# Reordering the seam between linear attention and a mixture of experts: gathers, u-term sums, copies and logits

## The chip, the cores and the metric

The kernel runs on one core of a Trainium2 chip. A core has TensorE (PE in the profile, its weight loads PEld), VectorE (DVE), ScalarE (ACT), GpSimd (POOL) and SyncE (SP), each with its own queue of instructions, and 16 DMA engines. The metric is the device time of one execution in microseconds. The times of the kernel before are 598.85, 599.25 and 601.51 us, the median 599.25.

## What is computed

A linear attention over 4 batches, 8 heads, 768 steps and 48 channels makes 3072 tokens of width 384; these go through a mixture of 8 experts, two of them for each token. Cut to what matters:

```python
for t in range(S):                                    # attention, w and u per head and channel
    cur = einsum('bhd,bhe->bhde', u * k_t, v_t)       # the u-term
    y[:, :, t] = einsum('bhd,bhde->bhe', r_t, state + cur)
    state = w * state + einsum('bhd,bhe->bhde', k_t, v_t)
x = y.transpose(0, 2, 1, 3).reshape(B * S, H * D)     # 3072 x 384

noisy = x @ w_gate + log1p(exp(x @ w_noise)) * noise  # routing
top2 and their softmax weights per token
for e in range(8):                                    # each token through its two experts
    out[token] += weight * (relu(x[token] @ w1[e]) @ w2[e])
```

## The kernel before

**Attention.** The loop at L1329 runs over 24 tiles of 128 tokens (6 chunks of time by 4 batches). Tile i goes through `products` (POOL: the u-term product rku of tile i+1, L410 to L421, and the scaled keys kd of tile i+2, L402), `ystate` and `yout` (PE: state and value parts of py, L531; the logits of tile i-1, L569; from tile 13 on the u-term sums of tile i+1, L433), `kvup` and `zup_v` (the state), `uterm_b` (DVE: the u-term sum c, L444 or L442, and its product cv with the values), `xout` (DVE: x = py + cv, L560, and its store to DRAM, xd), `turn_kr` (PE: turns of k and r of tile i+2, L225; DVE rT, ACT kT), `scores` (PE: PAB, L476), `turn_x` (PE turns x into KX, L225; ACT copies it to xT, L470) and `mask` (DVE: am, L484).

**Routing.** The logits are read in two groups of 12 tiles. A generator `route(g)` makes the top two, their slots and gates in some hundred small DVE steps; `steps(n)` and, later, `rstep(us)` issue a few of these between the other work, so where they are called sets the order on DVE, ACT and PE. Lists of token rows come from small PE matmuls (`place`, L709) behind two ACT scalings (L700); `rstep` counts down two calls from a list's making: the scaling at the first, the matmuls at the second. `rows` turns a list into row numbers GR (L883 to L885). `maybe_early`, at the end of a tile, does this for the first three token tiles of expert 0 once group 0 is routed, and `xgather` at once issues three indirect DMAs on POOL that gather them (L1020). All engines run their queue in order, so what stands behind a gather on POOL waits for it.

**Experts.** At the last tile `xT_first` (L1057) turns the three gathered tiles on PE (into RV, PAB and RT), with `turn_x` of tile 23 between the second and third, and then makes all three ACT copies xh (L1076) and three DVE remainders xl (L1078). `p1` is the first product of a chunk (ph, 8 blocks of 9 matmuls, L1132, with ACT and DVE making hb and ht, L1136 and L1138), `p2` the second (pym, L1168). Expert 0's first chunk is `p1(0, 0)`: its first four matmuls are issued at L1389, then `pl_alone` issues the logits of tile 23 into pl (L569), then the rest follows. The second chunk of expert 0 (s = 1 at L1469) carries the last routing steps: after each block of nine matmuls `rstep(STEPS_L0)`, then `wstep`, a step of the weight loading. Expert 1's gathers (list_1, L1432) and its turns (ptm, L1049) follow from these. From about 200 us on the experts follow each other with no routing between them.

Of the kernel before, what the change touches and what calls it, by code (L numbers as in the profile page):

```python
# [35 lines left out]
STEPS_L0 = 0.9  # L36
# [20 lines left out]
def kernel(  # L57
# [999 lines left out]
    def xT_first(between):  # L1057
        xh = moe.tile([128, ND, WMAX], F32R, name="xh")
        xl = moe.tile([128, ND, WMAX], F32R, name="xl")
        XH[0, 0] = (xh, xl)  # L1060
        part = lambda x, t: by_row(x[:, :, t * 128:(t + 1) * 128])
        whole = RT[:, :ND * 128].rearrange("p (d t) -> p d t", d=ND)
        ts = []
        for t, dst in zip(chunks(0)[0], (RV, PAB, None)):
            if dst is None:
                between()
            for d in range(ND):
                xg = XG[0, t][:, d * 128:(d + 1) * 128]
                if dst is None:
                    nc.tensor.transpose(whole[:, d, :], xg, ident)  # L1070
                else:
                    turn_rows(dst, d * 64, xg)
            ts.append((t, whole, xh[:, :, t * 128:(t + 1) * 128], xl[:, :, t * 128:(t + 1) * 128]) if dst is None else
                      (t, halves_of(dst, 0, ND), part(xh, t), part(xl, t)))
        for _, x, h_, l_ in ts:
            nc.scalar.activation(h_, x, AF.Copy)  # L1076
        for t, x, h_, l_ in ts:
            nc.vector.tensor_sub(l_, x, h_.bitcast(F32))  # L1078

# [30 lines left out]

    nph = [0]

    def p1(e, ci):
        w_ = sum(tw(t) for t in chunks(e)[ci])
        xh, xl = XH[e, ci]
        wh, wl = W[e][0]
# [5 lines left out]
        for f in range(NF):  # L1122
# [7 lines left out]
                q.sort(key=lambda z: z[1] is xl)  # L1130
            for j, (a, x, d) in enumerate(q):
                nc.tensor.matmul(ph[:, :w_], a[:, d, fs], x[:, d, :w_], start=(j == 0), stop=(j == len(q) - 1))  # L1132
                if nph[0] == 1 and j == 3:
                    yield
            for h_, a, b in parts:
                nc.scalar.activation(h_[:, f, 0, :], ph[:, a:b], AF.Relu)  # L1136
            for h_, a, b in parts:
# [157 lines left out]
                return  # L1295
            credit[0] -= c or 0.25

    def early(g):
        rows(EARLY[g] // 128, EARLY[g + 1] // 128, rows_of(g))
        xgather(0, g, g)  # L1300

    def route_when_done(i):
        for g, (a, b) in enumerate(GROUPS):
# [17 lines left out]

    def maybe_early():
        if 0 in routed and not late_mm and not early_done:
            early(0)
            early_done.append(1)

    early_done = []
    flag = consts_c()
    for i in range(NT):  # L1329
        products(i)  # L1330
        if i + 5 < NT:
            load(i + 5, (0, 2))
        if i in (4, 6):
# [16 lines left out]
        uterm_c(i, CV_EARLY, H)  # L1350
        steps(2)
        tick()
        if i + 1 < NT:
            uterm_b(i + 1)
        steps(1)
        xout(i)
        while i == I_EARLY and not early_done:
            rstep(1)
            maybe_early()
        if i == NT - 1:  # L1360
            logits_out(i - 1)
            route_when_done(i - 1)
            steps(3)
            xT_first(lambda: turn_x(i))
            p1a = p1(0, 0)
        else:
            turn_kr(i + 2)
            if i:
                logits_out(i - 1)
                route_when_done(i - 1)  # L1370
            uterm_c(i + 1, 0, CV_EARLY)
            steps(1)
            scores(i + 1)
            turn_x(i)
            tick()
            steps(1)
            mask(i + 1)
            steps(3)
            maybe_early()
        if not i:  # L1380
# [5 lines left out]
    psm[0] = ps_pool(ps_left, "psm", "left")  # L1386
    att_stack.close()
    hbp[0] = stack.enter_context(tc.tile_pool(name="hbp", bufs=1, side="right", reuse_waits="tile"))
    next(p1a)  # L1389
    ps_right.close()  # L1390
    psr[0] = ps_pool(ps_right, "psr", "right")

# [76 lines left out]
    for s in range(1, len(seq)):  # L1469
# [11 lines left out]
            xh_, xj_ = xD(*seq[s + 1]) if not end else ([], [])  # L1481
        else:
            xt = xT(*seq[s + 1])
        for j, _ in enumerate(p1(e, ci)):
            while hold and (s > 1 or listed):
                emit_out(*hold.pop(0))
            if s == 1:
                rstep(STEPS_L0)
                wstep()
                continue  # L1490
            if s > 2:
# [164 lines left out]
```

## Time and profile before

| | before |
|---|---|
| median of three | 599.25 us |
| the profiled execution | 599.14 us |
| its span, first to last instruction | 597.40 us |
| busy in the span: PE, PEld, DVE, ACT, POOL | 572.5, 547.3, 347.0, 284.8, 277.9 us |
| mean granted TensorE clock | 0.982 |

The rows quoted below are from that profiled execution, and times in them are microseconds from the span's start. A timeline row gives start, length, engine, line, operation, output<-inputs, shapes and count, and in brackets the idle time before it with what ended it. The attention ends and the experts start at about 136 us. A line without an entry in brackets followed its predecessor with hardly a gap.

### The profile page before, as it was taken

Reading aid. Unit: us, or ns where it says so; the run is one execution under the profiler, and the core shown is the slowest. Engines: PE = TensorE matmul, PEld = TensorE weight load, DVE = VectorE, ACT = ScalarE, POOL = GpSimd, SP = SyncE. Lnnn points to the kernel's source line nnn. Section 1 sums busy time; section 2 is a strip of 40 time slices with the busy share of each in tenths; the row PEclk is TensorE's granted clock in tenths of the full one; section 3 lists DMA queues with packets and bytes.
Section 4 is the critical chain, followed back from the end, with each engine's and each line's share of the span. In section 5 each row is a group of like instructions: output and inputs, shape, how many; then the busy total and the mean of one; then the engine's idle time right before and its main releaser. Section 6 shows DMA issues by size and latency. Waiting matters only on the chain.

```text
span 597.4 us, 13911 instructions
## 1 busy us (share of the span) xinstructions
PE 572.5 (96%) x5383; PEld 547.3 (92%) x5384; DVE 347.0 (58%) x788; ACT 284.8 (48%) x712; POOL 277.9 (47%) x416
## 2 busy tenths in 40 slices
PE   8899899969999999999999999999999999999995
PEld 5899888858898999999999999999999999999995
DVE  5998798837766455546454645455454546455331
ACT  4358777823263443554445545554554454445220
POOL 8998656640243743345352633344343516333222
PEclk9899999968999999999999999999999999999998
DMA  9998998219332661775654645565756455434211
GB/s 172 203 220 175 225 220 204 73 54 279 103 110 67 201 220 53 161 217 135 146 170 116 184 115 166 130 183 108 182 124 176 143 146 154 139 93 84 67 35 41
DMA packets 143225, 86.53 MB, mean 145 GB/s; under 512 B 118624, under 2 KB 133215, under 8 KB 143152
## 3 DMA queue, kind: packets, MB, share of 16 engines
q1 hardware_dynamic: 132368, 56.76, 39.6%
q0 software_dynamic: 10160, 28.81, 15.9%
q8 instruction: 44, 0.72, 0.5%
q14 instruction: 29, 0.24, 0.1%
q10 hardware_dynamic: 624, 0.00, 0.1%
HBM read 58.81 MB, written 19.86 MB: 132 GB/s over the span
## 4 chain that ended last, share of the span: by engine, by line
PE 86%; DVE 5%; issue 4%; POOL 3%; ACT 1%; DMA 1%; POOLq 0%; ACTq 0%; DVEq 0%
PE ph L1132 34%; PE pym L1168 32%; PE py L531 5%; PE PAB L476 3%; PE KX L225 2%; PE pym L1161 2%; PE pym L1159 2%; PE py L569 1%; DVE am L484 1%; POOL GT L1027 1%; PE RV L494 1%; PE RV L225 1%; PE RV L182 1%; PE ptm L1049 1%; DVE x L560 1%
## 5 line engine op out<-in xcount | busy, mean ns | idle before, releaser
L1168 PE MATMUL pym<-w1h,hb 128*128 128x384 f32 x768 | 200.4, 337 | 0.0
L1168 PEld LDWEIGHTS pym<-w1h,hb 128*128 128x128 f32 x768 | 139.4, 188 | 0.2
L1138 DVE SCALAR_TENSOR_TENSOR hb<-ph,hb 128x384 fp32r<-128x384 f32 x128 | 71.2, 556 | 117.4 <-ACT ht L1136 76.1
L1132 PE MATMUL ph<-xh,w0h 128*128 128x384 f32 (+1 forms) x384 | 136.2, 355 | 1.3 <-ACT xh L1076 1.3
L1132 PE MATMUL ph<-xh,w0l 128*128 128x384 f32 (+1 forms) x384 | 135.5, 353 | 0.0
L1132 PE MATMUL ph<-xl,w0h 128*128 128x384 f32 (+1 forms) x384 | 129.8, 352 | 0.0
L1168 PE MATMUL pym<-w1l,hb 128*128 128x384 f32 x384 | 129.2, 337 | 0.0
L1136 ACT ACTIVATE hb<-ph 128x384 fp32r<-128x384 f32 x128 | 62.9, 491 | 105.4 <-PE ph L1132 105.3
L1193 POOL DMA_INDIRECT out_dram<-ot,TK x56 | 60.3, 1076 | 105.7 <-DVE ot L1187 55.0
L1020 POOL DMA_INDIRECT xg<-xd,GR x56 | 60.7, 1083 | 59.1 <-DVE r_e L603 25.9
L1132 PEld LDWEIGHTS ph<-xh,w0h 128*128 128x128 f32 x384 | 72.5, 189 | 5.0 <-ACT xh L1076 1.6
L1132 PEld LDWEIGHTS ph<-xh,w0l 128*128 128x128 f32 x384 | 72.6, 189 | 3.1
L1132 PEld LDWEIGHTS ph<-xl,w0h 128*128 128x128 f32 x384 | 72.1, 188 | 3.3
L1168 PEld LDWEIGHTS pym<-w1l,hb 128*128 128x128 f32 x384 | 72.1, 188 | 0.1
L1035 POOL DMA_INDIRECT pv<-out_dram,GA x49 | 48.8, 997 | 48.3 <-DMA out_dram<-ot,TK 35.6
L1106 ACT ACTIVATE xh<-xj 128x384 fp32r<-128x384 f32 (+1 forms) x42 | 21.1, 502 | 43.8 <-DVE xj L1104 43.5
L1176 ACT ACTIVATE ot<-pym 128x384 f32<-128x384 f32 x42 | 20.4, 486 | 40.6 <-PE pym L1168 33.8
L1107 DVE TENSOR_TENSOR xl<-xj,xh 128x384 fp32r<-128x384 f32 (+1 forms) x42 | 22.4, 534 | 24.8 <-ACT xh L1106 24.8
L1092 ACT ACTIVATE pl<-xg 128x768 uint16<-128x768 uint16 (+1 forms) x42 | 35.3, 841 | 0.9 <-DMA xd<-pl 0.9
L484 DVE TENSOR_TENSOR am<-PAB,mneg 128x512 int32<-128x512 int32 x48 | 30.8, 683 | 5.3 <-PE PAB L476 5.0
L476 PE MATMUL PAB<-rT,kT 64*128 64x128 f32 x384 | 28.7, 286 | 2.9 <-issue 2.5
L402 POOL TENSOR_TENSOR kd<-kt,tabk 128x192 f32<-128x192 f32 x46 | 28.1, 631 | 4.9 <-DMA kt<-in_k_dram 2.1
(276 smaller groups left out, 837.6 us busy)
## 6 DMA issues: line engine op xcount, KB each, us to landing
stg<-in_moe_w_dram SPq DMA_DIRECT2D x24, 512.0 KB, 4.6
stg<-in_moe_w_dram SPq DMA_DIRECT2D x32, 384.0 KB, 3.4
xd<-x SPq DMA_DIRECT2D x24, 196.0 KB, 3.5
rd<-in_r_dram SPq DMA_DIRECT2D x24, 192.0 KB, 4.3
vt<-in_v_dram SPq DMA_DIRECT2D x24, 192.0 KB, 4.4
out_dram<-ot SPq DMA_DIRECT2D x16, 288.0 KB, 4.2
kt<-in_k_dram SPq DMA_DIRECT2D x23, 192.0 KB, 4.0
xg<-xd,GR POOLq DMA_INDIRECT x56, 3.1
```

The source lines that it names most:

```text
L402: nc.gpsimd.tensor_mul(KD[i][:, h], kt[i][:, h], tabk[:, h, :D])
L476: nc.tensor.matmul(pa[:, s, p, :], kT[i][s * 64:(s + 1) * 64, p, :], rT[i][s * 64:(s + 1) * 64, p, :], start=True, stop=True)
L484: nc.vector.tensor_tensor(am[:, :, h].bitcast(I32), pa[:, :, h].bitcast(I32), mneg[:, None].to_broadcast([128, 2, NP // 2, 128]), op=ALU.b ...
L531: nc.tensor.matmul(o[qs], lhsT[:, qs], rhs, start=first[q], stop=last, skip_group_check=True)
L1020: nc.gpsimd.indirect_dma_start(out=xg[:n, :XW if e else DM], out_offset=None, in_=xd[:rows_of(early_)], in_offset=bass.IndirectOffsetOnAxi ...
L1035: nc.gpsimd.indirect_dma_start(out=pv[:n], out_offset=None, in_=out, in_offset=bass.IndirectOffsetOnAxis(ap=GA[:n, e * NJ + t:e * NJ + t + ...
L1092: nc.scalar.activation(pl[:n], XG[e, t][:n, :DM].bitcast(U16).rearrange("p (d two) -> p two d", two=2), AF.Copy)
L1132: nc.tensor.matmul(ph[:, :w_], a[:, d, fs], x[:, d, :w_], start=(j == 0), stop=(j == len(q) - 1))
L1136: nc.scalar.activation(h_[:, f, 0, :], ph[:, a:b], AF.Relu)
L1138: nc.vector.scalar_tensor_tensor(h_[:, f, 1, :], ph[:, a:b], 0.0, h_[:, f, 0, :].bitcast(F32), op0=ALU.max, op1=ALU.subtract)
L1168: nc.tensor.matmul(py, hb[:, f, a, hs], x[:, f, :], start=(j == 0), stop=(j == len(q) - 1))
L1193: st = nc.gpsimd.indirect_dma_start(out=out, out_offset=bass.IndirectOffsetOnAxis(ap=TK[:n, q:q + 1], axis=0), in_=ot[:n], in_offset=None, ...
```

## The change

Five edits, all of order:

- `maybe_early` makes the row numbers only; the three early gathers are issued after `products` of the next tile (tile 22 here).
- `uterm_b` of tile 1 stands behind `mask` of tile 1, not ahead of `xout` of tile 0. All other tiles keep their place.
- In `xT_first` each ACT copy xh is issued right behind its tile's turns.
- `next(p1a)` is gone: the logits of tile 23 come before the first matmul of `p1(0, 0)`.
- `p1` takes a call `mid`, made behind the fifth of nine matmuls. For s = 1 it is half a routing step, and the step at the block's end is halved too.

```diff
-        for _, x, h_, l_ in ts:
-            nc.scalar.activation(h_, x, AF.Copy)
+            nc.scalar.activation(ts[-1][2], ts[-1][1], AF.Copy)
...
-    def p1(e, ci):
+    def p1(e, ci, mid=lambda: None):
...
-                if nph[0] == 1 and j == 3:
-                    yield
+                if j == 4:
+                    mid()
...
-    def early(g):
-        rows(EARLY[g] // 128, EARLY[g + 1] // 128, rows_of(g))
-        xgather(0, g, g)
...
-            early(0)
+            rows(EARLY[0] // 128, EARLY[1] // 128, rows_of(0))
             early_done.append(1)
...
         products(i)
+        if early_done and (0, 0) not in XG:
+            xgather(0, 0, 0)
...
-        if i + 1 < NT:
+        if i and i + 1 < NT:
             uterm_b(i + 1)
...
+        if i == I_EARLY and (0, 0) not in XG:
+            xgather(0, 0, 0)
...
             mask(i + 1)
+            if not i:
+                uterm_b(i + 1)
...
-    next(p1a)
...
-        for j, _ in enumerate(p1(e, ci)):
+        for j, _ in enumerate(p1(e, ci, lambda: rstep(STEPS_L0 / 2)) if s == 1 else p1(e, ci)):
...
             if s == 1:
-                rstep(STEPS_L0)
+                rstep(STEPS_L0 / 2)
```

On POOL at the end of tile 21 and the start of tile 22, the difference of the two orders (kd are scaled keys, xg<-xd the three early gathers, w1l the low half of expert 0's second weights, rku the u-term product of tile 23):

```order
 L421 TENSOR_TENSOR rku<-rT,kT 128x256 x2
 L402 TENSOR_TENSOR kd_101<-kt,tabk 128x4x48 x2
+L359 TENSOR_TENSOR w1l_1337<-stg,w1h_1336 128x384
+L421 TENSOR_TENSOR rku<-rT,kT 128x256 x2
 L1020 DMA xg<-xd,GR 128x384 x3
-L359 TENSOR_TENSOR w1l_1337<-stg,w1h_1336 128x384
-L421 TENSOR_TENSOR rku<-rT,kT 128x256 x2
 L356 TENSOR_TENSOR w1l_1337<-stg,w1h_1336 128x384
 L359 TENSOR_TENSOR w1l_1337<-stg,w1h_1336 128x384
```

The gathers have moved behind one weight half and the rku of tile 23; two weight halves stay behind them.

On ACT at the last tile, before (lg are logits, xT the turned tile 23, xh the copies of the gathered tiles):

```order
L578 ACTIVATE lg<-py 128x16
L470 ACTIVATE xT<-KX 128x2x3x64
L1076 ACTIVATE xh<-RV 128x2x3x64
L1076 ACTIVATE xh<-PAB 128x2x3x64
L1076 ACTIVATE xh<-RT 128x3x128
L578 ACTIVATE lg<-pl 128x16
```

and after:

```order
L578 ACTIVATE lg<-py 128x16
L1075 ACTIVATE xh<-RV 128x2x3x64
L1075 ACTIVATE xh<-PAB 128x2x3x64
L470 ACTIVATE xT<-KX 128x2x3x64
L1075 ACTIVATE xh<-RT 128x3x128
L578 ACTIVATE lg<-pl 128x16
```

The copy of tile 23 has moved behind two of the three xh copies. On PE the matmuls of pl (L569), which stood behind the first four of ph, now stand ahead of all of them.

On DVE at tile 0, the difference (z is the state, c and cv the u-term of tile 1, x of tile 0, rT of tile 2, am the mask of tile 1):

```order
 L504 TENSOR_TENSOR z_214<-RV,w_176 128x192
-L444 TENSOR_REDUCE c_365<-rku 128x8
-L448 TENSOR_TENSOR cv<-vt,c_365 128x384
 L560 TENSOR_TENSOR x_146<-py,cv 128x384
 L464 TENSOR_TENSOR rT<-RV,pwr 128x2x4x64
 L484 TENSOR_TENSOR am<-PAB,mneg 128x2x256 x2
+L444 TENSOR_REDUCE c_406<-rku 128x8
+L448 TENSOR_TENSOR cv<-vt,c_406 128x384
```

The sum and the product of tile 1 have moved behind the x of tile 0 and the mask of tile 1. The order of SP is the same in both.

## Rows read from the trace of the kernel before

**Rows 1.** Windows: stretch, length; busy (instructions) PE PEld DVE ACT POOL; PEclk, DMA share, GB/s.

```profile
16.40:20.00 3.60, 3.49 (x66) 3.33 (x66) 3.56 (x9) 0.49 (x1) 3.60 (x7) 0.54 1.02 220
...
119.73:125.41 5.68, 0.00 (x1) 0.00 (x0) 0.21 (x2) 0.46 (x3) 4.78 (x6) 0.74 0.37 104
125.41:132.70 7.29, 7.21 (x100) 6.91 (x101) 3.86 (x12) 2.90 (x11) 2.57 (x3) 0.50 0.08 30
132.70:136.20 3.50, 2.03 (x41) 1.53 (x39) 2.00 (x7) 1.82 (x5) 0.00 (x0) 0.99 0.33 67
136.20:139.50 3.30, 3.25 (x19) 2.70 (x20) 1.16 (x4) 0.18 (x1) 0.00 (x0) 0.50 1.00 282
139.50:151.30 11.80, 11.80 (x72) 11.64 (x71) 11.08 (x43) 3.44 (x7) 0.00 (x0) 1.00 0.97 300
```

**Rows 2.** Waits of PE over the span: us in total, times, longest.

```profile
PE py L433 <- POOL rku L421: 5.7, 1, 5.7
PE KX L225 <- DVE x L560: 3.3, 3, 2.5
...
PE ptm L1049 <- DMA xg<-xd,GR: 1.2, 1, 1.2
```

**Rows 3.** POOL timeline at tile 22, and the landing times of all gathers.

```profile
119.99 1.15 POOL L1020 DMA_INDIRECT xg<-xd,GR  x1 [4.29 <-DVE r_e L600]
...
122.71 0.94 POOL L1020 DMA_INDIRECT xg<-xd,GR  x1 [0.30 <-issue]
...
124.63 1.40 POOL L421 TENSOR_TENSOR rku<-rT,kT 128x256 f32<-128x256 f32 x2
...
DMA to landing us min/median/max: 2.9/3.1/6.3
```

**Rows 4.** DVE timeline from tile 22 to the last x, with one POOL row.

```profile
117.05 0.69 DVE L464 TENSOR_TENSOR rT<-RV,pwr 128x512 f32<-128x512 f32 x1
...
128.28 0.37 DVE L603 SCALAR_TENSOR_TENSOR r_e<-r_e,r2r 128x12 f32<-128x12 f32 x2
...
130.87 1.17 DVE L603 SCALAR_TENSOR_TENSOR r_e<-r_e,r2r 128x12 f32<-128x12 f32 x2
131.01 1.00 POOL L359 TENSOR_TENSOR w1l<-stg,w1h 128x384 fp32r<-128x384 f32 x1 [4.03 <-ACT w1h L357]
...
133.44 0.56 DVE L560 TENSOR_TENSOR x<-py,cv 128x384 f32<-128x384 f32 x1 [0.52 <-PE py L531]
```

**Rows 5.** Timeline of the copies and the first product of expert 0.

```profile
134.03 0.18 ACT L578 ACTIVATE lg<-py 128x16 f32<-128x16 f32 x1 [1.97 <-DVE x L560]
...
134.94 0.48 ACT L1076 ACTIVATE xh<-RV 128x384 fp32r<-128x384 f32 x1
...
135.68 0.51 ACT L1076 ACTIVATE xh<-RT 128x384 fp32r<-128x384 f32 x1
136.25 0.69 PE L1132 MATMUL ph<-xh,w0h 128*128 128x384 f32 x1 [1.32 <-ACT xh L1076]
...
137.82 0.91 PE L569 MATMUL pl<-wg,xT 128*64 128x64 f32 x12
```

**Rows 6.** Timeline of the start, DVE and POOL.

```profile
14.38 0.55 DVE L444 TENSOR_REDUCE c<-rku 128x8 f32<-128x384 f32 x1 [1.86 <-POOL rku L414]
...
15.78 0.55 DVE L560 TENSOR_TENSOR x<-py,cv 128x384 f32<-128x384 f32 x1
...
16.83 1.14 POOL L414 TENSOR_TENSOR rku<-rku,ub 128x192 f32<-128x192 f32 x2
...
20.51 0.54 DVE L560 TENSOR_TENSOR x<-py,cv 128x384 f32<-128x384 f32 x1
```

**Rows 7.** ACT timeline in the second product of expert 0.

```profile
174.45 0.49 ACT L1136 ACTIVATE hb<-ph 128x384 fp32r<-128x384 f32 x1 [0.28 <-PE ph L1132]
...
176.29 0.49 ACT L1136 ACTIVATE hb<-ph 128x384 fp32r<-128x384 f32 x1 [0.29 <-PE ph L1132]
...
176.78 0.98 ACT L700 ACTIVATE r_ob<-r_ob,pcol 128x300 bf16<-128x300 bf16 x2
```

## The prediction

> **What bounds the kernel now.** I read four views in this order. The windows by stage come first [rows 1]: after about 200 us TensorE is busy without a gap to the tail, so only what delays its arrival there counts, and the windows show where it loses time before. The waits of TensorE [rows 2] name the places: 5.7 us at the u-term sum of tile 23 (L433) behind POOL, 3.3 us in three waits of the x turns for VectorE (2.5 of them in one, at the start), 1.2 us at the turns of expert 1 behind a gather. The timeline rows then show what stands in the queues at these places: POOL at tile 22 [rows 3], VectorE up to the last x [rows 4], the copies ahead of expert 0 [rows 5], the start [rows 6], and ScalarE in the second product of expert 0 [rows 7]. The profiled execution took 599.14 us (span 597.40), 0.11 below the median of 599.25; the sum is made against 599.14.
>
> The 5.7 us is dearer than it looks. TensorE stood still from 119.73 to 125.41, its granted clock fell meanwhile, and it worked at 0.50 (the 1.2 GHz level) through the whole next stretch, 7.29 us [rows 1]. A second low stretch (0.50 from 136.2 to 139.5) followed the sparse 132.7 to 136.2, where TensorE was busy only 2.03 of 3.50 us.
>
> **Gathers behind the next tile's products.** Now POOL issues three gathers from 119.99, the last starting at 122.71 and taking 0.94, then a w1l half (1.00, as in the like row of rows 4), then from 124.63 the u-term product rku of tile 23 (1.40 for two) [rows 3]; TensorE waits for that. In the new order the w1l half and rku stand ahead. POOL is free from 115.70 (4.29 of idle time ahead of 119.99), so w1l ends at 116.70; rT of tile 23 is there at 117.74 (117.05 and 0.69) [rows 4], so rku runs from about 117.75 to 119.2. TensorE asks for it at 119.73: the wait is gone, with 0.5 us of slack. The gathers themselves don't move, since they waited for their row numbers until 119.99 anyway and POOL is free then.
>
> What follows at full clock: TensorE went from 125.41 to the last x, which VectorE computed from 133.44 to 134.00 [rows 4]. Of the 8.0 us to 133.40, 7.29 ran at half clock with TensorE busy 7.21 of it; halved that is 3.65, plus the 0.7 us that already ran at full clock, 4.3. So the last x would start at 124.1 and end at 124.6, the bound from below. VectorE's mask and the copies between don't shrink with the clock; tile 23 needs one mask behind its scores. I take 0.3 for that: 124.9.
>
> POOL now has two w1l halves behind the gathers, at 123.65 to 125.65, beside VectorE's last gate steps, and this speaks against the change. Two of these steps took 0.37 us at 128.28, but 1.17 at 130.87, when a w1l half ran on POOL from 131.01 to 132.01 [rows 4]. Before, they cost nothing since TensorE was later still. After, they may put the last x up to 1.0 later; the 0.3 above holds the middle case, and the range holds the rest.
> The Trainium skill's GPSIMD Engine Reference (Specifications) says that GpSimd shares its SBUF interfaces with VectorE and contends with VectorE instructions that have two SBUF inputs. The trace agrees with that in the 1.17 us row; taken at its worst the rule would make the gain 0.7 smaller.
>
> **Copies tile by tile, logits ahead of the first product.** Now ScalarE does the logits copy at 134.03, when the last x is done, then xT and three xh copies, the last from 135.68 for 0.51; the first product starts at 136.25, 2.25 after the x [rows 5]. The new order lets the xh copies of tiles 0 and 1 go ahead of xT. The same five copies then run back to back: 0.2 for the logits, four at 0.37 apart (134.94 to 135.68 holds two such steps), and 0.14 for the last to finish: 1.85 after the x, 0.4 less. So the first product starts at 124.9 + 1.85, about 126.8. The gathers bound this from below: issue to landing was 3.1 us in the median [rows 3], so the third lands at 125.8, its turn and copy take 0.7, and the product could not start before 126.5. The twelve logits matmuls of 0.91 us, which stood between the fourth and fifth product matmul from 137.82 [rows 5], now run while ScalarE makes the last copy and cost nothing there; without that cover they cost up to 0.6.
>
> The 72 product matmuls ran from 136.25 to 151.30, 15.05 us with the logits and with 3.30 us at half clock [rows 1, 5]. Without the logits' 0.91 that is 14.14, of which 2.39 at half clock; halved, 12.9 at full clock. Whether the clock falls again is unknown: the sparse stretch would be 124.0 to 126.8, about as long as the one before the fall at 136.2, but with the logits in it and without the low stretch ahead of it. A fall costs half of 3.30, 1.65. I take half of that, 0.8, since neither end is nearer. The product ends at 126.8 + 12.9 + 0.8 = 140.5 in place of 151.30: **10.8 us gained**, between 9.3 and 12.0.
> What comes behind keeps its distance: the second routing chain starts from the last logits, which move with the product, and SP's order is unchanged.
>
> **Half steps in the second product.** In the product of expert 0's second chunk the routing steps are called twice per nine matmuls. Both list placements (L709, twelve small matmuls each) stand 13 matmuls earlier in TensorE's order (after 32 and 59 in place of 45 and 72). Nine 448-column matmuls take 1.84 us (hb copies at 174.45 and 176.29) [rows 7], so one is 0.204 and 13 are 2.65. The gathers of expert 1, which wait for the second placement, come about as much earlier less new stalls, so the 1.2 us wait of the turns (L1049) [rows 2] should go. The price: the placement now comes one half step behind its two scaling copies, five matmuls or 1.02 us after the previous product's end, while these copies end 1.47 us after the hb copy starts (176.29 to 177.76) [rows 7]. That is about 0.5 of waiting, twice: 1.0. Bounds 0 (if the copies run before hb) to 2.0; I take 1.0. Net **0.2 gained**.
>
> **Tile 1's u-term sums behind its mask.** The x of tile 0 stands on VectorE behind tile 1's sum and product; the sum waits 1.86 for POOL's rku and starts at 14.38, so the x runs only at 15.78 [rows 6]. TensorE stood for 2.5 us [rows 2] and then ran at 0.54 from 16.4 to 20.0 [rows 1]. After, nothing of this stands ahead of it, it fits into the 1.86 of idle time, and TensorE goes on near 14.0 (it has asked since 2.5 us before 16.5, when the x was done). But POOL is busy throughout and gives tile 2's u-term product at 17.97 (16.83 and 1.14) [rows 6], which the x of tile 1 now waits for in VectorE's order: 0.55 for the sum, about as much again for the product, so it starts at about 19.2 in place of 20.51 [rows 6]. So 1.3 of the 2.5 us survives; another 0.4 can come from the clock, which was low until 20. The input transfers run at a DMA share near 1.0 here [rows 1] and can give some back later. Bounds 0 and 1.7; **1.2 gained**, nearest to POOL's row.
>
> **Sum.** 10.8 + 0.2 + 1.2 = 12.2, so 599.14 - 12.2 = 586.9, and with the 0.11 to the median 587.0 us, 2.0% faster.
>
> **Rivals.** (1) The clock stays low for longer. It did so for 7.3 us of work after the first stall; if the sparse stretch ahead of the product brings a like case, 7.3 us at half clock cost 3.6 in place of the 0.8 counted, and the time is 589.8; with the start's gain lost too, 591.0. For it: the same turns and copies stood before the fall at 136.2. Against: the product ended that fall within 3.30 us. (2) The wait only changes its name: the gathers land late, and the first turns wait for DMA in place of POOL. At the slowest landing of any of the 56 gathers, 6.3 us, the third lands at 129.0 and the product starts at 129.7: 2.9 given back, 589.9. Against: their median is 3.1 [rows 3]. (3) Slower: low clock through both products of expert 0's first chunk. Each is some 12.9 at full clock, so 25.8 us of work at half clock lose 25.8 and the time is 612; it decides once more than 13 us of full-clock work falls in a low stretch. Against: the product itself raised the clock from 139.5 on [rows 1]. (4) The change does nothing: the early flag is set at another tile and the gathers stay ahead of rku, so only the 0.4 at the copies, the 0.2 and the 1.2 come, 597.4. Against: the order of POOL shows rku ahead. (5) Better: no fall of the clock, no new stalls at the placements, the start's whole 1.7: 584.4.
>
> **How the numbers follow.** Chances: the forecast with its own terms at either bound 0.72, (1) 0.10, (2) 0.07, (5) 0.05, (3) 0.02, (4) 0.04. The range reaches from (5) to just above (1): 584.0 to 591.5. Half a per cent, 3 us, is about what a measurement of this kernel can tell from no change. Forecast, (1), (2) and (5) are all faster by more: 0.94; (4) is within: 0.04; (3) is slower: 0.02.
>
> **What would show it.** In the new trace the wait of L433 for POOL should be gone, the first product should start 9 to 10 us earlier and end 9.3 to 12.0 earlier, and 125 to 133 should be at clock 1.0. The wait of L1049 should be gone and L709 should wait for the copies of L700 about 0.5 us twice. The first x turn should start near 14 us with tile 1's x near 19.2. The forecast is wrong if the first turns wait for the gathers by more than a microsecond, or if the gain at 151 us is smaller at 200 us.

## The result, and the profile after

| | before | after |
|---|---|---|
| median of four runs each | 599.13 us | 591.31 us |
| lowest to highest | 598.85 to 601.51 | 589.92 to 593.16 |
| ratio, with its 95% interval | | 0.9863 (0.9824 to 0.9901) |
| the profiled execution | 599.14 us | 589.92 us |
| its span | 597.40 us | 588.2 us |
| mean granted TensorE clock | 0.982 | 0.995 |

The forecast was 587.0 us. The median went down by 7.8 us and the profiled span by 9.2, where the sum had 12.2; the profiled execution of after is the fastest of its four. Three marks on TensorE's timeline split the 9.2: when it asks for the u-term sum of tile 23 (A), from there to the start of expert 0's second product (B), and from there to the first product of expert 1 (C). What follows took 394.8 us in both.

| us | before | after | gained | forecast |
|---|---|---|---|---|
| A: L433 of tile 23 asked for at | 119.73 | 118.97 | 0.76 | 1.2 |
| B: to the second product | 31.84 | 24.17 | 7.67 | 10.8 |
| C: to expert 1's first product | 50.98 | 50.29 | 0.69 | 0.2 |

TensorE's rows at these marks, of before and then of after (before asked for L433 at 125.41 less the wait in brackets; the row at 128.42 is the first product's start):

```profile
125.41 1.27 PE L433 MATMUL py<-uw,rku 128*64 128x2 f32 x16 [5.68 <-POOL rku L421]
151.57 0.42 PE L1168 MATMUL pym<-w1h,hb 128*128 128x384 f32 x1
202.55 0.34 PE L1132 MATMUL ph<-xh,w0h 128*128 128x384 f32 x1
```

```profile
118.97 0.60 PE L433 MATMUL py<-uw,rku 128*64 128x2 f32 x16
128.42 0.64 PE L1131 MATMUL ph<-xh,w0h 128*128 128x384 f32 x1
143.14 0.42 PE L1167 MATMUL pym<-w1h,hb 128*128 128x384 f32 x1
193.43 0.34 PE L1131 MATMUL ph<-xh,w0h 128*128 128x384 f32 x1
```

These are windows of after by stage, core 0 (busy time of PE, PEld, DVE, ACT and POOL, each with its count, then the granted clock, the DMA share and GB/s); they answer [rows 1].

```profile
16.40:20.00 3.60, 1.68 (x30) 1.51 (x30) 3.35 (x8) 0.73 (x2) 3.60 (x7) 1.00 1.07 233
119.00:126.00 7.00, 5.37 (x132) 4.73 (x128) 5.96 (x17) 3.38 (x14) 5.03 (x5) 1.00 0.39 115
126.00:132.00 6.00, 4.96 (x33) 4.59 (x34) 4.46 (x17) 2.19 (x7) 0.00 (x0) 0.72 0.73 186
132.00:143.00 11.00, 11.00 (x72) 10.84 (x72) 9.73 (x34) 3.26 (x8) 0.00 (x0) 1.00 0.98 304
```

TensorE no longer stands still at tile 23, and from 119 to 126 its clock is 1.00, where it was 0.50 after the old stall. But it is busy only 5.37 of 7.00 us there, and the clock falls behind that, to 0.72 over 126 to 132. What it waited for from 112 to 152 us (total, times, longest) answers [rows 2]:

```profile
PE KX L225 <- DVE x L560: 1.8, 1, 1.8
PE RT L709 <- ACT r_ob L700: 0.9, 2, 0.5
PE pl L569 <- ACT xT L470: 0.5, 1, 0.5
PE PAB L225 <- DMA xg<-xd,GR: 0.4, 1, 0.4
```

The 5.7 us for POOL at L433 is gone, and the gathers cost 0.4. The new wait is 1.8 us for the last x. Two timelines of after show why, first VectorE's, then POOL's (start, length, line, tile, shapes, count). VectorE's second row is the second of the two steps in its first row, by itself:

```profile
122.41 2.72 DVE L603 SCALAR_TENSOR_TENSOR r_e<-r_e,r2r 128x12 f32<-128x12 f32 x2
122.61 2.52 DVE L603 SCALAR_TENSOR_TENSOR r_e<-r_e,r2r 128x12 f32<-128x12 f32 x1
125.94 0.56 DVE L560 TENSOR_TENSOR x<-py,cv 128x384 f32<-128x384 f32 x1
```

```profile
117.29 1.43 POOL L421 TENSOR_TENSOR rku<-rT,kT 128x256 f32<-128x256 f32 x2 [1.23 <-DVE rT L464]
122.16 0.95 POOL L1020 DMA_INDIRECT xg<-xd,GR  x1 [0.30 <-issue]
123.12 1.02 POOL L356 TENSOR_TENSOR w1l<-stg,w1h 128x384 fp32r<-128x384 f32 x1
124.08 1.01 POOL L359 TENSOR_TENSOR w1l<-stg,w1h 128x384 fp32r<-128x384 f32 x1
```

Two gate steps of twelve columns take 2.72 us, where these two took 1.17 in the kernel before and a pair with POOL idle 0.37 [rows 4]. They end at 125.13; POOL's two halves of w1l end at 125.09. The second step is the held one, from 122.61 on, which is 0.51 ahead of the first half, with the third gather still on POOL. The last x stands four small steps behind them. From its end at 126.50 the copies go as planned: the first product starts at 128.42, 1.92 us later, and 7.8 us ahead of the kernel before [rows 5]. The second product starts behind its 72 matmuls, at 143.14.

The start, VectorE's two first x and TensorE's waits there, answers [rows 6]:

```profile
12.05 0.54 DVE L560 TENSOR_TENSOR x<-py,cv 128x384 f32<-128x384 f32 x1
19.04 0.54 DVE L560 TENSOR_TENSOR x<-py,cv 128x384 f32<-128x384 f32 x1
```

```profile
17.47 0.46 PE L225 MATMUL RV<-ident,rd 64*128 64x64 f32 x8 [1.23 <-DVE z L504]
19.73 0.40 PE L225 MATMUL KX<-ident,x 64*128 64x64 f32 x6 [0.85 <-DVE x L560]
```

The first x comes 3.73 us earlier and the second 1.47. TensorE's one wait of 2.49 us has become two behind it, of 1.23 and 0.85.

### The profile page after: what moved, and what is told of

It is laid out like the page before. It is cut to its first block, busy times and chain, and to the rows that moved or that the text cites. A ratio compares the mean times of both kernels' runs of the same rounds, so it can differ in the third digit from the quotient of the medians.

```text
span 588.2 us, 13907 instructions
## 1 busy us (share of the span) xinstructions
PE 568.2 (97%) x5383; PEld 543.4 (92%) x5384; DVE 348.1 (59%) x788; ACT 284.5 (48%) x712; POOL 280.0 (48%) x416
## 4 chain that ended last, share of the span: by engine, by line
PE 89%; DVE 5%; POOL 2%; issue 2%; ACT 1%; DMA 1%; POOLq 0%; ACTq 0%
PE ph L1131 37%; PE pym L1167 34%; PE py L531 4%; PE PAB L476 3%; PE pym L1160 2%; PE pym L1158 2%; PE KX L225 2%; PE py L569 1%; DVE am L484 1%; PE RV L494 1%; POOL kd L402 1%; PE RV L225 1%; PE RV L182 1%; PE RT L709 1%; PE ptm L1049 1%
## 5 line engine op out<-in xcount | busy, mean ns | idle before, releaser
L1020 POOL DMA_INDIRECT xg<-xd,GR x56 | 62.0, 1107 | 49.2 <-DVE r_e L603 24.4
L1035 POOL DMA_INDIRECT pv<-out_dram,GA x49 | 50.3, 1026 | 52.4 <-DMA out_dram<-ot,TK 39.7
L484 DVE TENSOR_TENSOR am<-PAB,mneg 128x512 int32<-128x512 int32 x48 | 30.8, 682 | 4.9 <-PE PAB L476 4.5
L453 ACT ACTIVATE cv<-vt,c 128x48 f32<-128x48 f32 x120 | 30.2, 324 | 0.2
```

Of the source, the lines that this page charges most:

```text
L453: nc.scalar.activation(CV[i][:, h, :], vt[i][:, h, :], AF.Copy, scale=C8[i][:, h, :])
L484: nc.vector.tensor_tensor(am[:, :, h].bitcast(I32), pa[:, :, h].bitcast(I32), mneg[:, None].to_broadcast([128, 2, NP // 2, 128]), op=ALU.b ...
L1020: nc.gpsimd.indirect_dma_start(out=xg[:n, :XW if e else DM], out_offset=None, in_=xd[:rows_of(early_)], in_offset=bass.IndirectOffsetOnAxi ...
L1035: nc.gpsimd.indirect_dma_start(out=pv[:n], out_offset=None, in_=out, in_offset=bass.IndirectOffsetOnAxis(ap=GA[:n, e * NJ + t:e * NJ + t + ...
```

## Experiments

They ran in a later session on three chips, where the kernel before took 602.4 to 603.2 us. Each kernel has one profiled execution, and it can lie off the median of its runs (c_after 599.49 against 596.35, e11 601.25 against 597.40, e9 590.96 against 595.85). The next table gives A, B and C as above, worked out from the starts on TensorE's timeline; "x to 2nd" is the part of B from the last x's end to the second product, and the last column the ratio to the kernel before with its interval. The sum of A, B and C and some 394.8 to 395.9 us is the span.

| kernel | A | B | x to 2nd | C | ratio |
|---|---|---|---|---|---|
| before, first session | 119.73 | 31.84 | 17.57 | 50.98 | |
| after, first session | 118.97 | 24.17 | 16.64 | 50.29 | 0.9863 (0.9824 to 0.9901) |
| before (c_before) | 121.39 | 29.94 | 16.20 | 55.28 | |
| after (c_after) | 122.37 | 25.06 | 16.55 | 55.46 | 0.9899 (0.9852 to 0.9947) |
| gathers alone (e1) | 120.10 | 26.27 | 17.63 | 55.25 | 0.9905 (0.9877 to 0.9934) |
| start alone (e2) | 121.04 | 29.91 | 16.21 | 55.36 | 0.9994 (0.9966 to 1.0023) |
| late lows (e3) | 119.63 | 23.23 | 15.37 | 55.66 | 0.9904 (0.9868 to 0.9940) |
| whole steps (e4) | 121.42 | 25.28 | 16.68 | 55.00 | 0.9894 (0.9862 to 0.9926) |
| filled ahead of the product (e6) | 122.51 | 24.39 | 15.89 | 55.46 | 0.9893 (0.9859 to 0.9927) |
| late lows and filler (e7) | 118.27 | 24.23 | 15.50 | 55.45 | 0.9910 (0.9881 to 0.9940) |
| without the start's edit (e8) | 121.06 | 23.68 | 15.19 | 53.02 | 0.9877 (0.9826 to 0.9927) |
| start filled (e10) | 119.73 | 23.66 | 15.17 | 56.37 | 0.9891 (0.9831 to 0.9951) |
| VectorE shifted (e11) | 122.34 | 25.14 | 16.65 | 56.11 | 0.9907 (0.9872 to 0.9941) |
| combined (e9) | 117.48 | 24.41 | 16.70 | 52.44 | 0.9899 (0.9864 to 0.9934) |

**The two kernels again.** Neither was edited.

> The kernel before, unchanged, looked at on the chip on which the next three run, since the kernel before took 603.2 us in the comparisons of the last four and 599.1 in the first. If VectorE's and ScalarE's waits of 1.4 to 2.7 us that no engine ends (ahead of the c copy of tile 23 and in the second product, in the four experiments) belong to the chip or the session, they are here too, at the second product at least. If they belong to the edits, they are not.

> The changed kernel, unchanged, as the measure for the next two. If the wait ahead of the c copy of tile 23 (2.1 us in place of 0.7 in three experiments) belongs to the chip or the session, its c copy comes 2.1 us after VectorE's last step before it, the first product starts about 8.0 us after the c copy, and the gain over the kernel before is about 1.4 us less than the 7.8 of the first comparison: near 1.0 per cent. If it belongs to the edits, the c copy comes after 0.7 and the ratio is again near 0.986.

The medians were 603.84 (one run) and 596.35 us. Both kernels lose some 4 to 5 us of C in the later session, so that much belongs to the chip or the session. The wait ahead of the c copy of tile 23 is there in c_after too. VectorE's rows of after and then of c_after (in brackets the idle time ahead):

```profile
120.11 0.17 DVE L442 COPY c<-py 128x8 f32<-128x8 f32 x1 [0.70 <-PE py L531]
```

```profile
124.90 0.17 DVE L442 COPY c<-py 128x8 f32<-128x8 f32 x1 [2.07 <-PE PAB L476]
```

The copy needs py alone. By the profile, which models the ends of matmuls, TensorE ended py at 120.07 in the first and at 123.48 in the second, so in c_after VectorE seems to stand 1.4 us for nothing. But the trace also keeps the times of the signals (semaphore events) by which one engine lets another go on. TensorE's signal for py is at 120.09 in after and at 124.87 in c_after, and the copy starts 0.02 us behind it in both. So it was TensorE's signal that came late. The next two are late as well: in c_after the one for the scores PAB comes at 127.13, 2.56 us behind their modelled end and 1.5 us after TensorE had begun the turn of x that stands behind them, and the one for that turn comes at 127.21, 1.14 us late. VectorE's mask waits for the first of them (1.26 us, in the row of L484 further down), ScalarE's copy xT for the second. In after all three come within 0.03 us. In all ten kernels of the later session that have the moved gathers the three are late by 1.4 to 1.5, 2.5 to 2.7 and 1.1 to 1.2 us. In c_before and e2, where POOL comes last ahead of that copy (7.69 us after VectorE's last step in c_before), they are on time.

**The gathers alone.** On the kernel before:

```diff
-            early(0)
+            rows(EARLY[0] // 128, EARLY[1] // 128, rows_of(0))
...
         products(i)
+        if early_done and (0, 0) not in XG:
+            xgather(0, 0, 0)
...
+        if i == I_EARLY and (0, 0) not in XG:
+            xgather(0, 0, 0)
```

> The kernel before with the move of the gathers alone; the start, the copies and the steps of the second product stay as before. The theory (the gain is the stall of L433 and the low clock behind it, capped by VectorE's gate steps that POOL's two w1l halves hold up) expects no wait at L433, the last x within 0.5 us of 127 (the changed kernel has its end at 126.5 and starts 0.7 us ahead), the first product's end about 1.5 us behind the changed kernel's 142.9, and a time near 592.5, that is 6.5 to 7 us of the 9.2. A rival (the order of the copies carries a third of the gain or more, since without it the clock falls for longer) expects 595 or more.

597.91 us, 0.9905 of the kernel before, beside 0.9899 for all edits together in that session. L433 of tile 23 waits for nothing, and B is 26.27 in place of 29.9 to 31.8. The last x ended at 128.74 and not at 127, 8.64 us behind A where after had 7.53: the late signals came on top (1.4 us at the c copy, 1.3 at the mask), while the gate steps, which now met one half alone, took 1.15. By the medians the move of the gathers carries nearly the whole gain. The rival that gave a third or more to the copies expected 595, which is 0.9931 of 599.13 and lies just inside the end of e1's interval, so the time alone doesn't put it out; the column "x to 2nd" gives the copies and the logits 1.0 us (below).

**The start alone.** On the kernel before:

```diff
-        if i + 1 < NT:
+        if i and i + 1 < NT:
             uterm_b(i + 1)
...
             mask(i + 1)
+            if not i:
+                uterm_b(i + 1)
```

> The kernel before with tile 1's u-term sums behind its mask, nothing else. The theory (0.7 us survive to tile 23, because the input transfers give half of it back between 25 and 60 us) expects the first x near 12 us, L433 of tile 23 asked for about 0.7 us earlier but its wait 0.7 longer where POOL is the one waited for, so 598.5 to 599.1. The prediction's 1.2 us expects 597.9. A rival (all is given back to the transfers by 60 us) expects the same arrival at tile 23 as before and 599.1.

603.69 us, 0.9994: no gain that shows. The 1.2 us of the prediction would be 0.9980, which the interval doesn't exclude. A was 121.04, only 0.35 ahead of c_before. The windows of three kernels (PE busy, granted clock, DMA share, GB/s) show where it went, start alone first, then without the start's edit, then with the start filled:

```profile
16.00:20.00 4.00, 1.96 (x38) 0.99 1.08 224
20.00:28.00 8.00, 7.32 (x124) 0.58 1.04 233
```

```profile
16.00:20.00 4.00, 3.91 (x74) 0.57 1.00 200
20.00:28.00 8.00, 7.70 (x210) 1.00 1.02 234
```

```profile
16.00:20.00 4.00, 3.71 (x45) 1.00 0.99 198
20.00:28.00 8.00, 7.70 (x198) 1.00 0.96 209
```

The edit moves the sparse stretch from ahead of 16.5 us to 16 to 20, and the low clock moves with it, from 16 to 20 into 20 to 28.

**Without the start's edit, and with its gaps filled.** Both on the changed kernel; the first takes back the diff above, the second is

```diff
+            if i == 1:
+                warm(4, RT)
             turn_kr(i + 2)
...
+            if i == 1:
+                warm(5, RT)
             turn_x(i)
```

> The changed kernel with tile 1's u-term sums back where they stood before; the rest is the changed kernel. The theory (on a chip where the second x waits 1.40 us the clock falls to 0.50 from 20 to 26 us, and the start's whole gain goes back) expects the first x near 16 us, the clock at 0.6 from 16 to 20 and at 1 behind it, L433 of tile 23 asked for at 121 to 121.5 as in the kernel before on the slower chip (121.4), which is 1 us ahead of the changed kernel there (122.4), and a time 0 to 1 us under the changed kernel's. The prediction (1.2 us from the start) expects 1.2 us more than the changed kernel's time.

> The changed kernel with nine added matmuls on zeros that nothing reads, in the two waits of TensorE in tile 1 (four ahead of the turns of tile 3, five ahead of the turn of tile 1's x). The theory (those idle stretches bring the clock down from 20 us on, and that eats the start's gain) expects the clock at 1.00 from 16 to 60 and L433 of tile 23 asked for 1.0 to 2.0 us earlier than the changed kernel's 122.4 on the slower chip, 120.4 to 121.4. The rival (input transfers set the pace from 25 to 60 us, whatever the clock) expects the clock at 1.00 and L433 asked for at 122 or later, with longer waits of TensorE between 25 and 60.

They took 596.01 and 596.99 us, neither apart from the changed kernel's 596.35. The first asked for L433 at 121.06, as its theory had it, the second at 119.73, with the clock at 1.00 from 16 to 60 us. Over all kernels A sorts by the clock. Of the eight with the start's edit and no filler, five had a clock of 0.58 to 0.79 in 20 to 28 us and A between 121.04 and 122.51, mean 121.9; three kept 1.00 and had 118.27 to 119.63. The filled one had 119.73. The five without the edit lie between 117.48 and 121.39, mean 119.95. So A is about 1 us earlier with the edit where the clock holds and 2 later where it falls (1.6 and 1.4 without e9, which has other matmuls at its very start). One profile each, with a spread of 4 us even among kernels alike, shows the direction and not the size.

**POOL's halves and VectorE's gate steps.** The last weight unit's low halves go to VectorE behind the last x:

```diff
                     part = [[x[:, z:z + m] for x in (t, *flat)] for z in (0, m)]
+                    if mat and c1 == NF:
+                        for p in part:
+                            yield
+                            nc.scalar.activation(p[1], p[0], AF.Copy)
+                        yield
+                        for p in part:
+                            nc.vector.tensor_sub(p[2], p[0], p[1].bitcast(F32))
+                        yield
+                        return
```

> The changed kernel with the last weight unit's two low halves taken from POOL and put on VectorE behind the last x and its xl subtractions. The theory (POOL's two w1l halves held VectorE's gate step of 12 columns for 2.5 us, and with it the last x) expects two L603 at 0.37 us together, the last x ending near 124.3 in place of 126.5, then the third gather's landing as the next bound, the first product starting near 126.8 in place of 128.4, and 1.6 us off the time. Rival one (the gather's own work on POOL or something else held VectorE) expects L603 still at 1 us or more and under 0.6 us gained. Rival two (the two halves, 0.55 us each on VectorE, come due ahead of the second routing chain) expects the placements L709 of the second product to wait 1 us and more, and no gain at 200 us.

The mask and the gate steps, VectorE's of e3 (where the added lines make L484 into L493, L603 into L612 and L560 into L569), then VectorE's and POOL's of c_after:

```profile
124.54 1.29 DVE L493 TENSOR_TENSOR am<-PAB,mneg 128x512 int32<-128x512 int32 x2 [1.31 <-PE KX L225]
125.75 0.36 DVE L612 SCALAR_TENSOR_TENSOR r_e<-r_e,r2r 128x12 f32<-128x12 f32 x2
126.93 0.56 DVE L569 TENSOR_TENSOR x<-py,cv 128x384 f32<-128x384 f32 x1
```

```profile
127.16 1.29 DVE L484 TENSOR_TENSOR am<-PAB,mneg 128x512 int32<-128x512 int32 x2 [1.26 <-PE KX L225]
128.36 1.15 DVE L603 SCALAR_TENSOR_TENSOR r_e<-r_e,r2r 128x12 f32<-128x12 f32 x2
```

```profile
126.54 1.00 POOL L356 TENSOR_TENSOR w1l<-stg,w1h 128x384 fp32r<-128x384 f32 x1
128.27 1.01 POOL L359 TENSOR_TENSOR w1l<-stg,w1h 128x384 fp32r<-128x384 f32 x1 [0.72 <-ACT w1h L357]
```

With nothing on POOL the two steps take 0.36 us, beside one half 1.15, beside two halves 2.72. So POOL's halves hold the steps. Rival one is out for that, but not for 0.51 us of the hold in after, which lie ahead of the first half, beside the third gather; in e3 the steps come 2 us after the last gather, so e3 says nothing of them. Against the gather, single steps of this kind in the last 0.4 us of an earlier gather took 0.16 (after, c_after, e1). What held the step in the 0.51 us isn't shown. From the c copy to the first product it was 7.20 us in e3 against 8.24 in c_after and 8.31 in after. The two 8.3 are not alike: the late signal holds the mask by 1.3 us in e3 and c_after and not in after, and because of it the steps of c_after, and of every kernel of the later session with the halves on POOL behind the moved gathers, met one half only (1.14 to 1.15). The hold of 2.72 was seen in one execution. B is the shortest of all, 23.23. The time doesn't show it: 597.75 us. The L709 groups waited 1.05 and 2.54 us in C, so this doesn't decide on rival two, since c_after waits there as long without it.

The Trainium skill's page "SBUF — State Buffer" (SBUF: two separate sides) says that the ports which GpSimd and VectorE share are an exclusive lock, for a VectorE instruction with two SBUF inputs against a GpSimd one that reads SBUF: who starts first holds them for its whole instruction, and the other blocks fully. The trace agrees where one half is met: in c_after the half started 0.09 us ahead of the steps, and the mask L484 above, one of whose inputs is in PSUM, took its usual 1.29 beside the other half. In after it agrees in part: the held step ended 0.04 us behind POOL's second half, but it had started 0.51 ahead of the first, where by this rule POOL would have waited.

**Filling the gap ahead of the first product.** On the changed kernel:

```diff
-            xT_first(lambda: turn_x(i))
+            xT_first(lambda: (warm(8, KX[:, 0]), turn_x(i)))
...
+    warm(3)
     pl_alone(NT - 1)
```

> The changed kernel with eleven added matmuls on zeros that nothing reads (eight of 512 columns ahead of the last x's turn, three ahead of the last logits), so that TensorE isn't idle for the 1.75 us in which it waits for the last x. The theory (the clock falls in the sparse stretch ahead of the first product, and the fall costs it 1.65 us) expects the granted clock at 1.00 from 120 to 152, the 72 product matmuls in 12.8 to 13.4 us in place of 14.4, and 1.0 to 1.6 us off the time. Rival one (the fall has nothing to do with this idle time) expects the clock below 1 in the first 3 us of the product again, and 14.4. Rival two (the added matmuls stand in the way) expects the turn of the last x later by 0.3 us or more, which eats a third of it.

Windows of c_after and then of e6 (PE busy, granted clock, DMA share, GB/s):

```profile
128.00:132.00 4.00, 2.71 (x65) 1.00 0.14 53
132.00:143.00 11.00, 10.70 (x62) 0.84 0.96 276
```

```profile
128.00:132.00 4.00, 4.00 (x70) 1.00 0.13 46
132.00:143.00 11.00, 11.00 (x77) 1.00 0.96 277
```

The clock stayed at 1.00 and the 72 matmuls took 13.22 us against 14.29. The added matmuls also put the turn of the last x 0.72 us behind the x's end, where it follows at once without them, so B gained 0.67. The time shows none of it (597.45). That is what the theory of the clock expects, and rival two took half of it. One profile doesn't settle it: e3 and e8 kept the clock from 124 to 143 us without the filler.

**Both.** The late halves, with one matmul in place of eight ahead of the turn:

```diff
+            xT_first(lambda: (warm(1, KX[:, 0]), turn_x(i)))
```

> The changed kernel with both: the last weight unit's low halves on VectorE behind the last x, and four added matmuls on zeros (one ahead of the last x's turn, three ahead of the last logits). The theory expects two L603 at 0.37 us, the first product starting 7.2 us after the c copy of tile 23 in place of 8.0 to 8.3, its 72 matmuls in 12.8 to 13.4 us at clock 1.00, and the time 1.5 to 2.5 us under the changed kernel's on the same chip. The rival (what is gained ahead of the first product is taken back by a wait in the second) expects less than 0.5 us.

596.89 us. The product took 13.18 us and the gate steps 0.37, as the theory had it. But here the clock was at 0.81 over 119 to 128, and the first product came 8.5 us after the copy and not 7.2.

**The half steps.** On the changed kernel:

```diff
-        for j, _ in enumerate(p1(e, ci, lambda: rstep(STEPS_L0 / 2)) if s == 1 else p1(e, ci)):
+        for j, _ in enumerate(p1(e, ci)):
...
-                rstep(STEPS_L0 / 2)
+                rstep(STEPS_L0)
```

> The changed kernel with the routing steps of the second chunk's product called once per nine matmuls at the full rate, as before; the rest is the changed kernel. The theory (the half steps are worth what the wait of the turns L1049 was, less no new stall) expects that wait back at 1.2 us and expert 1's first product 0.7 us later than in the changed kernel, that is near 194.3 in place of 193.6. The prediction's own sum (1.2 us removed, 1.0 added in two waits of the placements) expects 0.2 us of difference, 193.8. A rival (the half steps do nothing, the 0.7 comes from the earlier first product) expects 193.6.

597.89 us, C 55.00 against c_after's 55.46: no gain from the half steps in that session. TensorE's waits in C of e4, then of c_after (total, times, longest):

```profile
PE RT L709 <- ACT r_ob L700: 2.4, 4, 1.0
PE ph L1131 <- DVE ht L1137: 1.8, 1, 1.8
PE ptm L1049 <- DMA xg<-xd,GR: 1.2, 1, 1.2
```

```profile
PE RT L709 <- ACT r_ob L700: 4.6, 3, 3.7
```

The 1.2 us at the turns is back in e4 and gone in c_after, but a wait of 3.7 at one placement stands there instead; the sums are 5.4 and 4.6. In the first session the waits were 2.1 and 0.9, and C fell by 0.69.

**What stands ahead of the c copy.** Two attempts moved the programs against it. The first adds 24 memsets on VectorE:

```diff
         xout(i)
+        if 2 < i < 15:
+            for _ in range(2):
+                nc.vector.memset(pad, 0.0)
```

> The changed kernel with 24 added memsets of one element on VectorE, two in each of tiles 3 to 14, so that whatever VectorE runs afterwards stands 24 instructions further back in its program. If the wait of 2.1 us ahead of the c copy of tile 23 (no engine's work ends it; a transfer of instructions of 1.0 us is under way shortly before it ends) hangs on how far VectorE is in its program, it is gone there (0.7 us or less between TensorE's last u-term sum and the copy) and a like wait turns up about one tile earlier or not at all. If it hangs on the data or on another engine, it stays at 2.1 us. The time isn't expected to differ by over 1.5 us from the changed kernel's.

The copy's row of e11, and of e9 below (where it is L452):

```profile
124.84 0.17 DVE L442 COPY c<-py 128x8 f32<-128x8 f32 x1 [2.05 <-PE PAB L476]
```

```profile
120.00 0.17 DVE L452 COPY c<-py 128x8 f32<-128x8 f32 x1 [2.07 <-PE PAB L486]
```

It stays. So TensorE's late signal doesn't hang on how far VectorE is in its program, nor, by e9, TensorE. A transfer of instructions (0.02 MB, 1.0 us) started 0.7 to 1.8 us ahead of the copy in the later session, and in after one started 0.2 us behind it. What holds the signal stays open.

**Combined.** On the changed kernel, with the start's edit taken back, the late halves, `warm(3)` ahead of the last logits, and

```diff
-    warm(WARM0, RV[:, 0])
+    for z in range(4 * WARM0):
+        nc.tensor.matmul(RV[:, 0, z % 4 * 128:z % 4 * 128 + 128], wsrc, wsrc, start=True, stop=True)
```

> The changed kernel with what the runs so far point to: tile 1's u-term sums back where they stood before; the last weight unit's low halves on VectorE behind the last x; three added matmuls on zeros ahead of the last logits; and the nine matmuls of 512 columns on zeros at the very start cut into 36 of 128 columns, so that everything on TensorE stands 54 instructions further back in its program. The theory on the low halves expects two L603 at 0.37 us and the first product starting 7.2 us after the c copy of tile 23, and the clock at 1.00 in its 72 matmuls, 12.8 to 13.5 us. If the wait of 2.1 us ahead of that c copy hangs on how far TensorE is in its program, the copy now comes about 1.2 us after TensorE's last u-term sums began and the second product starts near 142.8; if not, 2.6 us after and near 144.2 (the changed kernel on this slower chip: 147.4). The time then is 593.5 or 595.0 at a median of the kernel before of 602.4 to 603.2, that is 0.985 or 0.987 of it. A rival (the waits for ScalarE in the second product, 2.8 to 3.7 us in all runs on this chip, set the pace behind it) expects no gain over the changed kernel's 596.4.

595.85 us, 0.9899, the same as the changed kernel there. The profiled execution was the lowest of the session at 590.96 us, with A at 117.48 and the first product 7.20 us after the copy at clock 1.00. Inside the product a new wait came: TensorE's rows of e9,

```profile
134.08 0.44 PE L1141 MATMUL ph<-xh,w0h 128*128 128x384 f32 x1 [0.27 <-DVE hb L1147]
136.50 0.44 PE L1141 MATMUL ph<-xh,w0h 128*128 128x384 f32 x1 [0.57 <-DVE hb L1147]
```

VectorE has the second routing chain's small steps between its hb there, with the two halves ahead of them, and the 72 matmuls took 14.69 us at full clock. The median is what the rival expected, no gain; but its reason isn't shown, since C was 3.0 us shorter than in c_after. No kernel here beats the changed one by more than the runs spread.

## Why the prediction was right, and where its steps were not

**The stall at L433** went as said: rku from 117.29, no wait, full clock until 126. The gathers cost TensorE 0.4 us, so rival (2) is out. Alone, this edit gave 0.9905 (e1).

**The last x** was forecast 5.17 us after L433 is asked for (119.73 to 124.9) and came after 7.53. The step that failed is the price of POOL's two halves beside the gate steps: 0.3 taken, 1.0 as the bound, 2.35 measured (2.72 less 0.37). The row of [rows 4] from which it came had one half beside the steps; with the gathers ahead, both halves were ready and ran one after the other, and the step was held through both, and for 0.51 us ahead of them that no run explains. Without the halves the pair takes 0.36 (e3). The bound of 1.0 rests on one half, and one half is what the steps met in the later session, where the mask came 1.3 us later: 0.8 (1.15 less 0.36).

**Copies and logits** were forecast at 1.3 us (0.4 and 0.91). The column "x to 2nd" gives it, with the clock fallen and not: 17.6 against 16.6 (before and e1 against after, c_after, e4, e11), and 16.2 against 15.2 (c_before and e2 against e8 and e10). That is 1.0 both times. The 1.85 us to the first product (its terms add up to 1.82) measured 1.92.

**The clock ahead of the product.** Half of 1.65 was counted, 0.8. The same column gives a fall 1.4 us, and it came in the profile of after and in some of those of the later session, of one and the same code around it: c_before kept the clock where before lost it. Filled, it held in three of three (e6, e7, e9), unfilled in five of eleven; in e7 and e10 it had fallen ahead of the product instead (0.64 and 0.70 over 124 to 128). Without a fall the 72 matmuls took 13.2 to 13.5 us, not 12.9. Half was a fair price for a thing that happens in about half of the executions; the profiled one paid it all. Rival (1), 3.6 us, is out.

**The half steps** were forecast at 0.2 net: 1.2 removed, 1.0 of new waits. In the first session the 1.2 went and the new waits did not come, 0.69 gained; in the later one 3.7 us of waiting came in one piece and C was no shorter (c_after, e4). The mechanism was right for what was removed. The new waits were mis-sized: the two scalings do end 1.47 us after the hb copy starts, but the placement begins with what the first of them gives (in after that one signals at 173.52 and the placement begins at 173.56). The 3.7 us of the later session stand behind a late signal of TensorE for which ScalarE waits (last section).

**The start** was forecast at 1.2 from the arrival of the second x, at 19.2 (19.04 measured), and 0.76 reached tile 23. Over the later session nothing did (e2, 0.9994). The step that failed is the clause that put the clock on the gain's side (0.4 could come from it): the sparse stretch moves behind the first x and takes the low clock with it, in five of eight profiles. The give-back to the input transfers was in the bounds; no run here took the transfers apart from the clock.

**The signs.** The prediction expected the first product to start 9 to 10 us earlier and to end 9.3 to 12.0 earlier, the clock at 1.0 from 125 to 133, and L709 to wait 0.5 us twice more. Measured are 7.8, 8.4, a clock of 0.72 from 126 to 132, and the same 0.9 us of L709 before and after. The x turn near 14 us (13.43), the missing wait of L1049 and a gain at 200 us no smaller than at 151 came as said.

**The sum.** 12.2 forecast, 9.2 in the profile and 7.8 in the medians. The profile's difference of 3.0 is 2.4 at the last x and 1.0 in the product, with 0.4 at the start, less 0.5 at the half steps and some 0.3 in rounding and the step to the second product. The 591.31 us lie 0.2 below the upper end of the range, and for other reasons than the one that set that end: it was rival (1)'s long low clock, and it should have been the 2.4 us of the held steps and a whole fall of 1.4. That the range holds them is luck to that extent. Rivals (3) and (4) are out by the clock of 1.00 from 132 on and by rku ahead of the gathers on POOL, and (5) by the fall (its own terms give 584.7, not 584.4).

## What to carry to other kernels

When an instruction is moved, list what runs on the engines that share ports with the one that is now ahead of the critical result, and price it as a block for its whole length, with every such instruction in a row, not by the one row in which one of them stood there before. A gain that ends in an idle TensorE can move the low clock along: look at what the clock does behind the new gap before counting the old one as won. Read an edit's worth between two marks on the critical engine; here the time of a run moves by 2 us for other reasons, and edits worth 1 us showed between marks and not in the medians. Where an engine seems to stand idle behind a finished matmul, look for TensorE's signal: the end of a matmul in the profile is modelled.

## What was not expected of the hardware

- A VectorE step of twelve columns, 0.17 us alone, took 2.52 us beside the end of a gather and two POOL instructions of 1.0 us each, until 0.04 us behind the second's end.
- In the later session some of TensorE's signals came late, by 1.1 to 3.6 us behind the modelled ends of the matmuls in c_after, and the engines that wait for them stood: VectorE 1.4 us at the c copy and 1.3 at the mask in all ten kernels with the moved gathers, and ScalarE ahead of an hb copy in the first product of expert 0's second chunk (the row below, of c_after: modelled end 170.21, signal 173.84), with TensorE's placement behind it held 3.73 us. C is 50.3 to 51.0 us in the two profiles of the first session and 52.4 to 56.4 in the twelve of the later one. What made the signals late, the traces don't show.
- The same code kept the full clock in one execution and fell to half in another (the first product of before and c_before), at a price of 1.4 us.

ScalarE's row of c_after, with the idle time ahead and what the profile puts it down to:

```profile
173.87 0.49 ACT L1135 ACTIVATE hb<-ph 128x384 fp32r<-128x384 f32 x1 [2.72 <-remote]
```
